# Feed-forward of a hash-attention block: units in a written issue order, without GpSimd

## The chip, the cores and the metric

The kernel runs on one core of a Trainium2 chip. The metric is the device time of one execution in microseconds (us). The core has TensorE (PE, matrix products; PEld is its loading of weights), VectorE (DVE), ScalarE (ACT), GpSimd (POOL) and SyncE (SP), each with its own queue of instructions that it runs in order. SBUF is the memory that all engines work on, PSUM the one that TensorE writes its products to.

## The reference

Four batches of eight heads, 768 positions of 64 numbers. Each query and each key gets a 6-bit bucket from the signs of a projection, and a query attends only to keys of its own bucket. The result `x` of 3072 rows x 512 goes through a feed-forward of 2048 columns:

```python
h = x @ w_in                      # 3072 x 512 @ 512 x 2048
sp = np.maximum(h, 0.0) + np.log1p(np.exp(-np.abs(h)))
g = h * erf(sp)
return (g @ w_out).astype(np.float32)   # @ 2048 x 512
```

## The kernel before

Everything is in float32. Attention comes first (lines 85 to 374): for each head and each 128 queries `attend` makes scores, maximum, exponential and normalized weights, `turn` transposes the weights on TensorE with the matrix `ident` and copies them out of PSUM on ScalarE, and `weigh` multiplies with the values and writes `xT`, the transposed input of the feed-forward, which stays in SBUF. The weights `w_in` and `w_out` come in meanwhile and stay in SBUF too.

The feed-forward (from line 376) takes the rows in 12 tiles of T = 256, and each tile's 2048 columns in NG = 4 groups of 512. One tile and group is a *unit* `u`; there are NU = 48. All tiles of a unit's arithmetic are 128 partitions x 1024 numbers. The steps of a unit, by function:

- `hidden` (L391): the first product, 16 products of 128 x 256 into `h_ps`, a PSUM tile of two banks. The trace has two records for each product, so 32 records.
- `take` (L406): ScalarE copies `h_ps` to `h` (L410), which frees the PSUM buffer; VectorE makes `e` = |h| (L411).
- `exponential` (L419): ScalarE `e` = exp(-e) (L423), VectorE `w` = (e + 1) - 1 (L424).
- `softplus` (L428): ScalarE `s` = Ln(e + 1) (L433), GpSimd `w` = e - w (L434, what the rounding of e + 1 lost), VectorE `s` = max(h, 0) + s (L435) and `s` = min(s, 4) + w (L438).
- `polynomial` (L442): erf is written as a Tanh of a polynomial, a product of three factors. ScalarE squares `s` into `z` (L446), then for each factor squares `z` plus a constant from `cq` (L450), and VectorE adds a constant and multiplies (L451).
- `gate` (L457): ScalarE Tanh (L460), GpSimd `h` = h * tanh (L461).
- `project` (L465): the second product. For a tile and 128 of its rows (`tt` 0 or 1), `half` says which two groups are added into `o_ps`: 8 products, 16 records, of 128 x 512. After the second half VectorE copies the result out (L480) and SyncE sends it to memory.

The first product has two PSUM buffers of two banks (`ps_h`), the second four of one bank (`ps_o`). They lie where attention's PSUM pools lay: `ps_sc` (scores, two of two banks), `ps_t` (transposes and hash bits, three banks) and `ps_av` (one bank).

The loop over pairs of units (L491 on) writes `hidden`, `project`, `take` and `polynomial` of the pair before, then `exponential`, `gate`, `softplus`. This text order is only a priority. A planner, which holds an estimated duration for each operation, decides at compile time in which order each engine issues what is ready, so a later unit's step can stand ahead of an earlier one's. ScalarE loads a table of functions (ACT_TABLE_LOAD) when a function is not in the one loaded; in the trace Ln needs another one than exp and Tanh, and copy and square need none.

Of the kernel before, what the change touches and what calls it, by code (L numbers as in the profile page):

```python
# [29 lines left out]
F32 = mybir.dt.float32  # L33
# [3 lines left out]
AF = mybir.ActivationFunctionType  # L37
ALU = mybir.AluOpType
AX = mybir.AxisListType
PSUM = bass.MemoryType.PSUM  # L40

P = 128
# [4 lines left out]
ERF_LEAD = 1.418517747371711e-07  # L47
ERF_Q = (
    (6.2794604751645355, 19.35174303303216),
    (-5.316226701641483, 239.37499811839012),  # L50
    (-20.943483610527835, 66.98472325796595),
)
# [3 lines left out]
def kernel(  # L56
# [11 lines left out]
    nc = tc.nc  # L68
# [10 lines left out]
    T = 256  # L79
    G = 4  # L80
    NG = NF // G
    TPB = S // T
    scale = 1.0 / D**0.5
    assert D == 64 and S == 768 and DM == H * D and NT == B * S and 1 << (NB2 // 2) == P - D

    const = ctx.enter_context(tc.tile_pool(name="const", bufs=1))
    ident = const.tile([P, P], F32, name="ident")
    make_identity(nc, ident)
    proj_sb = const.tile([P, NB2], F32, name="proj_sb")
    powers_f = const.tile([NB2, 2 * D], F32, name="powers_f")  # L90
    powers_b = const.tile([NB2, 2 * D], BF16, name="powers_b")
# [22 lines left out]
    ]  # L114

    with (
        tc.tile_pool(name="load", bufs=4) as load,
        tc.tile_pool(name="bitp", bufs=2) as bitp,
        tc.tile_pool(name="ep", bufs=4) as ep,
# [5 lines left out]
        tc.tile_pool(name="ps_t", bufs=3, space=PSUM) as ps_t,  # L125
        tc.tile_pool(name="ps_av", bufs=1, space=PSUM) as ps_av,
    ):
        heads = {}

        def fetch(i):  # L130
# [219 lines left out]
        for n in range(NH * NC + 3):  # L350
# [16 lines left out]
            w = n - 3  # L367
# [4 lines left out]
            t = n - 2  # L372
# [3 lines left out]
    cq = const.tile([P, len(ERF_Q)], F32, name="cq")  # L376
    for j, (c, _) in enumerate(ERF_Q):
        nc.vector.memset(cq[:, j : j + 1], c)

    hp = ctx.enter_context(tc.tile_pool(name="hp", bufs=8))  # L380
    ew = ctx.enter_context(tc.tile_pool(name="ew", bufs=2))
    sp = ctx.enter_context(tc.tile_pool(name="sp", bufs=4))
    work = ctx.enter_context(tc.tile_pool(name="work", bufs=2))
    outp = ctx.enter_context(tc.tile_pool(name="outp", bufs=2))
    ps_h = ctx.enter_context(tc.tile_pool(name="ps_h", bufs=2, space=PSUM))
    ps_o = ctx.enter_context(tc.tile_pool(name="ps_o", bufs=4, space=PSUM))

    NU = (NT // T) * NG
    st = {}

    def hidden(u):  # L391
        t, g = divmod(u, NG)
        b, t0 = t // TPB, (t % TPB) * T
        ps = ps_h.tile([P, G, T], F32, name="h_ps", tag="h")
        for f in range(G):
            for kc in range(NK):
                nc.tensor.matmul(  # L397
                    out=ps[:, f, :],
                    lhsT=w_in_sb[:, kc, (g * G + f) * P : (g * G + f + 1) * P],
                    rhs=xT[b][:, kc, t0 : t0 + T],  # L400
                    start=(kc == 0),
                    stop=(kc == NK - 1),
                )
        st[u] = dict(ps=ps)

    def take(u):  # L406
        d = st[u]
        h = d["h"] = hp.tile([P, G, T], F32, name="h", tag="h")
        e = d["e"] = ew.tile([P, G, T], F32, name="e", tag="e")
        nc.scalar.copy(out=h, in_=d.pop("ps"))  # L410
        nc.vector.tensor_scalar(  # L411
            out=e[:, :, :].bitcast(I32),
            in0=h[:, :, :].bitcast(I32),
            scalar1=0x7FFFFFFF,
            scalar2=None,
            op0=ALU.bitwise_and,
        )

    def exponential(u):  # L419
        d = st[u]  # L420
        e = d["e"]
        w = d["w"] = ew.tile([P, G, T], F32, name="w", tag="w")
        nc.scalar.activation(out=e, in_=e, func=AF.Exp, scale=-1.0)  # L423
        nc.vector.tensor_scalar(  # L424
            out=w, in0=e, scalar1=1.0, scalar2=-1.0, op0=ALU.add, op1=ALU.add
        )

    def softplus(u):  # L428

        d = st[u]  # L430
        h, e, w = d["h"], d.pop("e"), d.pop("w")
        s = d["s"] = sp.tile([P, G, T], F32, name="s", tag="s")
        nc.scalar.activation(out=s, in_=e, func=AF.Ln, bias=1.0)  # L433
        nc.gpsimd.tensor_tensor(out=w, in0=e, in1=w, op=ALU.subtract)  # L434
        nc.vector.scalar_tensor_tensor(  # L435
            out=s, in0=h, scalar=0.0, in1=s, op0=ALU.max, op1=ALU.add
        )
        nc.vector.scalar_tensor_tensor(  # L438
            out=s, in0=s, scalar=S_MAX, in1=w, op0=ALU.min, op1=ALU.add
        )  # L440

    def polynomial(u):  # L442
        d = st[u]
        p = d.pop("s")
        z = work.tile([P, G, T], F32, name="z", tag="z")
        nc.scalar.activation(out=z, in_=p, func=AF.Square)  # L446
        for j, (_, r) in enumerate(ERF_Q):
            last = j == len(ERF_Q) - 1
            q = z if last else work.tile([P, G, T], F32, name=f"q{j}", tag=f"q{j}")
            nc.scalar.activation(out=q, in_=z, func=AF.Square, bias=cq[:, j : j + 1])  # L450
            nc.vector.scalar_tensor_tensor(  # L451
                out=q, in0=q, scalar=r, in1=p, op0=ALU.add, op1=ALU.mult
            )
            p = q
        d["p"] = p

    def gate(u):  # L457
        d = st[u]
        p = d.pop("p")
        nc.scalar.activation(out=p, in_=p, func=AF.Tanh, scale=ERF_LEAD)  # L460
        nc.gpsimd.tensor_tensor(out=d["h"], in0=d["h"], in1=p, op=ALU.mult)  # L461

    o_live = {}

    def project(t, half, tt):  # L465

        if half == 0:
            o_live[tt] = ps_o.tile([P, DM], F32, name="o_ps", tag="o")
        ps = o_live[tt]
        for f in range(half * NF // 2, (half + 1) * NF // 2):  # L470
            nc.tensor.matmul(  # L471
                out=ps,
                lhsT=st[t * NG + f // G]["h"][:, f % G, tt * P : (tt + 1) * P],
                rhs=w_out_sb[:, f, :],
                start=(f == 0),
                stop=(f == NF - 1),
            )
        if half == 1:
            ob = outp.tile([P, DM], F32, name="ob", tag="ob")
            nc.vector.tensor_copy(out=ob, in_=ps)  # L480
            r0 = t * T + tt * P
            nc.sync.dma_start(out=out[r0 : r0 + P, :], in_=ob)
        if tt == 1:
            for g in range(half * NG // 2, (half + 1) * NG // 2):
                st.pop(t * NG + g)

    NB = NU // 2
    for k in range(NB + 2):
        for j in range(2):
            if k < NB:  # L490
                hidden(2 * k + j)  # L491
            if k >= 2:
                project((k - 2) // 2, (k - 2) % 2, j)
            if k < NB:
                take(2 * k + j)
            if 1 <= k <= NB:
                polynomial(2 * (k - 1) + j)
        for j in range(2):
            if k < NB:
                exponential(2 * k + j)  # L500
        for j in range(2):
            if 1 <= k <= NB:
                gate(2 * (k - 1) + j)
        for j in range(2):
            if k < NB:
                softplus(2 * k + j)


# [51 lines left out]
```

## Time and profile before

| | us |
|---|---|
| Median of 3 runs | 1537.13 |
| Lowest and highest | 1536.66 and 1537.61 |
| The profiled execution | 1537.1 |
| Its span (first to last instruction) | 1535.3 |
| Mean granted clock of TensorE | 0.985 |

| Engine | busy us | share of the span |
|---|---|---|
| PE | 1435.7 | 94% |
| PEld | 805.3 | 52% |
| DVE | 1080.8 | 70% |
| ACT | 874.9 | 57% |
| POOL | 379.0 | 25% |

Shares over the whole span mix attention and feed-forward, which have different limits; a table by stage separates them. "Idle before, releaser" behind a row says how long the engine stood still before that work and what ended its wait. [...] Several instructions of one kind in a row are merged into one line with their count (x32).

### The profile page before, as it was taken

Reading aid. Unit: us, or ns where it says so; the run is one execution under the profiler, and the core shown is the slowest. Engines: PE = TensorE matmul, PEld = TensorE weight load, DVE = VectorE, ACT = ScalarE, POOL = GpSimd, SP = SyncE. Lnnn points to the kernel's source line nnn. Section 1 sums busy time; section 2 is a strip of 40 time slices with the busy share of each in tenths; the row PEclk is TensorE's granted clock in tenths of the full one; section 3 lists DMA queues with packets and bytes.
Section 4 is the critical chain, followed back from the end, with each engine's and each line's share of the span. In section 5 each row is a group of like instructions: output and inputs, shape, how many; then the busy total and the mean of one; then the engine's idle time right before and its main releaser. Section 6 shows DMA issues by size and latency. Waiting matters only on the chain.

```text
span 1535.3 us, 14770 instructions
## 1 busy us (share of the span) xinstructions
PE 1435.7 (94%) x5248; PEld 805.3 (52%) x5248; DVE 1080.8 (70%) x1772; ACT 874.9 (57%) x1249; POOL 379.0 (25%) x198
## 2 busy tenths in 40 slices
PE   7999999999999999999997999989898999998986
PEld 3444444444444444544575666656565656565552
DVE  6888878888786676676638766666666665665673
ACT  2444444444444454454548877676767776676764
POOL 3333323332220000000014433333232323323231
PEclk9999999999999999999998999999999999999998
DMA  5222222222211011010000000000000000000000
GB/s 154 80 64 67 67 74 81 70 67 64 67 36 42 26 37 41 26 37 6 1 0 1 7 7 14 7 7 14 1 14 7 7 14 1 14 7 7 14 7 20
DMA packets 40705, 49.19 MB, mean 32 GB/s; under 512 B 27308, under 2 KB 27320, under 8 KB 40632
## 3 DMA queue, kind: packets, MB, share of 16 engines
q1 hardware_dynamic: 35856, 31.47, 6.9%
q0 software_dynamic: 4608, 16.78, 3.5%
q8 instruction: 41, 0.67, 0.2%
q14 instruction: 32, 0.26, 0.1%
q10 hardware_dynamic: 168, 0.01, 0.0%
HBM read 41.96 MB, written 6.29 MB: 31 GB/s over the span
## 4 chain that ended last, share of the span: by engine, by line
PE 37%; DVE 27%; ACT 26%; issue 7%; POOL 2%; DMA 1%; POOLq 0%; SPq 0%; DVEq 0%; ACTq 0%
PE av L332 13%; PE sc L274 11%; DVE s L435 7%; PE tr_ps L317 7%; ACT q L450 5%; DVE s L438 3%; ACT e L423 3%; ACT z L446 3%; DVE m L282 3%; ACT L433 3%; DVE q L451 2%; ACT h L410 2%; PE bits_ps L225 2%; ACT L460 2%; ACT s L433 2%
## 5 line engine op out<-in xcount | busy, mean ns | idle before, releaser
L397 PE MATMUL h_ps<-xT,w_in_sb 128*128 128x256 f32 x1536 | 349.0, 386 | 44.1 <-ACT h L410 43.9
L471 PE MATMUL o_ps<-w_out_sb,h 128*128 128x512 f32 x768 | 344.3, 602 | 22.4 <-POOL h L461 22.4
L397 PEld LDWEIGHTS h_ps<-xT,w_in_sb 128*128 128x128 f32 x1536 | 293.6, 193 | 115.9 <-ACT h L410 69.9
L324 ACT COPY eT<-tr_ps 128x384 f32<-128x384 f32 x384 | 171.0, 481 | 319.2 <-PE tr_ps L317 317.8
L274 PE MATMUL sc<-ka,qa 128*128 128x384 f32 x768 | 299.0, 498 | 11.0 <-ACT e L289 10.3
L332 PE MATMUL av<-eT,vt 128*64 128x384 f32 x768 | 261.6, 490 | 0.0
L471 PEld LDWEIGHTS o_ps<-w_out_sb,h 128*128 128x128 f32 x768 | 148.1, 193 | 192.5 <-issue 164.5
L434 POOL TENSOR_TENSOR w<-e,w 128x1024 f32<-128x1024 f32 x48 | 114.7, 2389 | 487.1 <-DVE w L424 487.1
L282 DVE TENSOR_REDUCE m<-sc 128x1 f32<-128x768 f32 x192 | 183.2, 954 | 64.5 <-PE sc L274 61.4
L289 ACT ACTIVATE e<-sc,nm 128x768 f32<-128x768 f32 x192 | 173.9, 906 | 90.4 <-DVE nm L284 87.9
L461 POOL TENSOR_TENSOR h<-h,z 128x1024 f32<-128x1024 f32 x48 | 119.8, 2497 | 357.2 <-ACT z L460 357.2
L317 PEld LDWEIGHTS tr_ps<-ident,e 128*128 128x128 f32 x1152 | 126.2, 140 | 120.5 <-issue 50.6
L317 PE MATMUL tr_ps<-ident,e 128*128 128x128 f32 x1152 | 176.9, 281 | 7.2 <-DVE e L302 2.4
L332 PEld LDWEIGHTS av<-eT,vt 128*64 128x64 f32 x768 | 99.8, 137 | 153.2 <-issue 145.2
L274 PEld LDWEIGHTS sc<-ka,qa 128*128 128x128 f32 x768 | 126.5, 192 | 69.1 <-ACT e L289 25.4
L435 DVE SCALAR_TENSOR_TENSOR s<-h,s 128x1024 f32<-128x1024 f32 x48 | 118.5, 2468 | 37.2 <-ACT s L433 37.2
L446 ACT ACTIVATE z<-s 128x1024 f32<-128x1024 f32 x48 | 50.7, 1056 | 157.6 <-DVE s L438 157.6
L451 DVE SCALAR_TENSOR_TENSOR q<-q,s 128x1024 f32<-128x1024 f32 x48 | 62.8, 1308 | 91.3 <-ACT q L450 91.3
L302 DVE TENSOR_SCALAR e<-e,r 128x768 f32<-128x768 f32 x192 | 124.3, 648 | 2.8
L424 DVE TENSOR_SCALAR w<-e 128x1024 f32<-128x1024 f32 x48 | 66.7, 1389 | 73.4 <-ACT e L423 73.4
L450 ACT ACTIVATE q<-z,cq 128x1024 f32<-128x1024 f32 x96 | 105.1, 1140 | 1.4
L339 DVE COPY xT<-av 64x384 f32<-64x384 f32 x64 | 35.3, 551 | 92.6 <-PE av L332 92.5
(44 smaller groups left out, 1227.2 us busy)
## 6 DMA issues: line engine op xcount, KB each, us to landing
qa<-in_qkT_dram SPq DMA_DIRECT2D x32, 384.0 KB, 3.4
raw<-in_w_in_dram POOLq DMA_DIRECT2D x16, 512.0 KB, 4.2
raw<-in_w_out_dram POOLq DMA_DIRECT2D x16, 512.0 KB, 3.8
ka<-in_qkT_dram SPq DMA_DIRECT2D x32, 192.0 KB, 3.8
vt<-in_v_dram SPq DMA_DIRECT2D x32, 192.0 KB, 2.5
out_dram<-ob SPq DMA_DIRECT2D x24, 256.0 KB, 2.0
powers_f<-in_powers_dram ACTq DMA_DIRECT2D x1, 6.0 KB
proj_sb<-in_proj_dram SPq DMA_DIRECT2D x1, 6.0 KB, 1.7
```

The costliest lines, as they stand in the source:

```text
L274: nc.tensor.matmul(out=sc[:, half, 0:HS], lhsT=d["qa"][:, c * P : (c + 1) * P], rhs=d["ka"][:, half * HS : (half + 1) * HS], start=True, s ...
L282: nc.vector.reduce_max(out=m, in_=sc[:, :, 0:HS], axis=AX.XY)
L289: nc.scalar.activation(out=e[:, :].rearrange("p (h k) -> p h k", h=2), in_=sc[:, :, 0:HS], func=AF.Exp, bias=nm[:, 0:1], scale=scale, accu ...
L302: nc.vector.tensor_scalar(out=e, in0=e, scalar1=r[:, 0:1], scalar2=None, op0=ALU.mult)
L317: nc.tensor.transpose(out=ps[:, j * P : (j + 1) * P], in_=e[:, kc * P : (kc + 1) * P], identity=ident,)
L324: nc.scalar.copy(out=dst, in_=src)
L332: nc.tensor.matmul(out=av[rows, :], lhsT=d["vt"][:, kc, :], rhs=d["eT"][:, kc, :], start=(kc == 0), stop=(kc == NC - 1),)
L397: nc.tensor.matmul(out=ps[:, f, :], lhsT=w_in_sb[:, kc, (g * G + f) * P : (g * G + f + 1) * P], rhs=xT[b][:, kc, t0 : t0 + T], start=(kc = ...
L435: nc.vector.scalar_tensor_tensor(out=s, in0=h, scalar=0.0, in1=s, op0=ALU.max, op1=ALU.add)
L450: nc.scalar.activation(out=q, in_=z, func=AF.Square, bias=cq[:, j : j + 1])
L461: nc.gpsimd.tensor_tensor(out=d["h"], in0=d["h"], in1=p, op=ALU.mult)
L471: nc.tensor.matmul(out=ps, lhsT=st[t * NG + f // G]["h"][:, f % G, tt * P : (tt + 1) * P], rhs=w_out_sb[:, f, :], start=(f == 0), stop=(f ...
```

## The change

1. `ident` moves from the pool that stays to a pool `one` that is released with attention.
2. `e - w` and `h * tanh` move from GpSimd to VectorE; the first now stands in `exponential`, directly behind `w`.
3. `polynomial` takes both units of a pair, factor by factor. It multiplies into `s` in place, and `q1` shares its two buffers (tag `wq`) with `w`. `e`, `w`/`q1`, `z` and `q0` have two buffers each, `h` nine in place of eight, `s` five in place of four.
4. `ps_h` has three buffers (six banks), `ps_o` two.
5. The loop is written in periods `p` of one pair and stands in `manual_schedule()`: within it each engine issues its instructions in the order of the text. Where these fall among the instructions outside it (the end of attention) is still the planner's. A pair has its first products in period p (the second one's `take` follows in p+1), exponential and `softplus` in p+1, the polynomial in p+2, `gate` and `project` in p+3.

```diff
-    ident = const.tile([P, P], F32, name="ident")
-    make_identity(nc, ident)
...
+        tc.tile_pool(name="one", bufs=1) as one,
...
+        ident = one.tile([P, P], F32, name="ident")
+        make_identity(nc, ident)
...
-    hp = ctx.enter_context(tc.tile_pool(name="hp", bufs=8))
-    ew = ctx.enter_context(tc.tile_pool(name="ew", bufs=2))
-    sp = ctx.enter_context(tc.tile_pool(name="sp", bufs=4))
+    hp = ctx.enter_context(tc.tile_pool(name="hp", bufs=9))
+    sp = ctx.enter_context(tc.tile_pool(name="sp", bufs=5))
...
-    ps_h = ctx.enter_context(tc.tile_pool(name="ps_h", bufs=2, space=PSUM))
-    ps_o = ctx.enter_context(tc.tile_pool(name="ps_o", bufs=4, space=PSUM))
+    ps_h = ctx.enter_context(tc.tile_pool(name="ps_h", bufs=3, space=PSUM))
+    ps_o = ctx.enter_context(tc.tile_pool(name="ps_o", bufs=2, space=PSUM))
...
+    NP = NU // 2
...
-        e = d["e"] = ew.tile([P, G, T], F32, name="e", tag="e")
+        e = d["e"] = work.tile([P, G, T], F32, name="e", tag="e")
...
-        w = d["w"] = ew.tile([P, G, T], F32, name="w", tag="w")
+        w = d["w"] = work.tile([P, G, T], F32, name="w", tag="wq")
...
+        nc.vector.tensor_tensor(out=w, in0=e, in1=w, op=ALU.subtract)
...
-        nc.gpsimd.tensor_tensor(out=w, in0=e, in1=w, op=ALU.subtract)
...
-    def polynomial(u):
-        d = st[u]
-        p = d.pop("s")
-        z = work.tile([P, G, T], F32, name="z", tag="z")
-        nc.scalar.activation(out=z, in_=p, func=AF.Square)
+    def polynomial(us):
+        for u in us:
+            st[u]["z"] = work.tile([P, G, T], F32, name="z", tag="z")
+            nc.scalar.activation(out=st[u]["z"], in_=st[u]["s"], func=AF.Square)
         for j, (_, r) in enumerate(ERF_Q):
-            last = j == len(ERF_Q) - 1
-            q = z if last else work.tile([P, G, T], F32, name=f"q{j}", tag=f"q{j}")
-            nc.scalar.activation(out=q, in_=z, func=AF.Square, bias=cq[:, j : j + 1])
-            nc.vector.scalar_tensor_tensor(
-                out=q, in0=q, scalar=r, in1=p, op0=ALU.add, op1=ALU.mult
-            )
-            p = q
-        d["p"] = p
+            for u in us:
+                z, s = st[u]["z"], st[u]["s"]
+                if j == 0:
+                    q = work.tile([P, G, T], F32, name="q0", tag="q0")
+                elif j == 1:
+                    q = work.tile([P, G, T], F32, name="q1", tag="wq")
+                else:
+                    q = z
+                nc.scalar.activation(out=q, in_=z, func=AF.Square, bias=cq[:, j : j + 1])
+                nc.vector.scalar_tensor_tensor(
+                    out=s, in0=q, scalar=r, in1=s, op0=ALU.add, op1=ALU.mult
+                )
...
-        p = d.pop("p")
-        nc.scalar.activation(out=p, in_=p, func=AF.Tanh, scale=ERF_LEAD)
-        nc.gpsimd.tensor_tensor(out=d["h"], in0=d["h"], in1=p, op=ALU.mult)
+        s = d.pop("s")
+        nc.scalar.activation(out=s, in_=s, func=AF.Tanh, scale=ERF_LEAD)
+        nc.vector.tensor_tensor(out=d["h"], in0=d["h"], in1=s, op=ALU.mult)
...
-    def project(t, half, tt):
-
+    def project(k, tt):
+
+        t, half = divmod(k, NG // 2)
...
-    NB = NU // 2
-    for k in range(NB + 2):
-        for j in range(2):
-            if k < NB:
-                hidden(2 * k + j)
-            if k >= 2:
-                project((k - 2) // 2, (k - 2) % 2, j)
-            if k < NB:
-                take(2 * k + j)
-            if 1 <= k <= NB:
-                polynomial(2 * (k - 1) + j)
-        for j in range(2):
-            if k < NB:
-                exponential(2 * k + j)
-        for j in range(2):
-            if 1 <= k <= NB:
-                gate(2 * (k - 1) + j)
-        for j in range(2):
-            if k < NB:
-                softplus(2 * k + j)
+    with tc.manual_schedule():
+        for p in range(NP + 3):
+            if p < NP:
+                hidden(2 * p)
+            if 1 <= p <= NP:
+                take(2 * p - 1)
+            if p >= 3:
+                gate(2 * p - 6)
+                gate(2 * p - 5)
+            if 1 <= p <= NP:
+                exponential(2 * p - 2)
+                exponential(2 * p - 1)
+                softplus(2 * p - 2)
+                softplus(2 * p - 1)
+            if p < NP:
+                take(2 * p)
+            if 2 <= p <= NP + 1:
+                polynomial((2 * p - 4, 2 * p - 3))
+            if p >= 3:
+                project(p - 3, 0)
+            if p < NP:
+                hidden(2 * p + 1)
+            if p >= 3:
+                project(p - 3, 1)
```

## Rows read from the trace of the kernel before

**Rows 1.** Busy time by stage (x instructions), last three: PEclk, DMA share, GB/s
```profile
784.00:1531.00 747.00, 680.54 (x2294) 439.72 (x2292) 489.08 (x359) 524.13 (x480) 234.44 (x96) 0.97 0.02 9
...
900.00:1000.00 100.00, 100.00 (x346) 65.36 (x344) 67.21 (x49) 68.90 (x64) 31.27 (x13) 1.00 0.02 8
1100.00:1200.00 100.00, 90.08 (x310) 58.21 (x309) 66.01 (x49) 67.32 (x62) 31.91 (x14) 1.00 0.03 11
```

**Rows 2.** Waits of PE from 776 us on: total, times, longest
```profile
PE h_ps L397 <- ACT h L410: 43.9, 28, 3.4
PE o_ps L471 <- POOL h L461: 22.4, 4, 8.8
```

**Rows 3.** Timeline of one round of the loop: start, us, engine, line
```profile
1079.35 0.99 ACT L410 COPY h<-h_ps 128x1024 f32<-128x1024 f32 x1
...
1080.39 7.17 PE L397 MATMUL h_ps<-xT,w_in_sb 128*128 128x256 f32 x32 [1.54 <-ACT h L410]
1081.06 0.69 DVE L411 TENSOR_SCALAR e<-h 128x1024 int32<-128x1024 int32 x1
...
1085.77 2.35 POOL L434 TENSOR_TENSOR w<-e,w 128x1024 f32<-128x1024 f32 x1 [0.63 <-DVE w L424]
1086.06 3.14 DVE L435 SCALAR_TENSOR_TENSOR s<-h,s 128x1024 f32<-128x1024 f32 x1 [0.36 <-ACT s L433]
...
1090.56 1.06 ACT L446 ACTIVATE z<-s 128x1024 f32<-128x1024 f32 x1 [4.54 <-DVE s L438]
...
1095.97 7.17 PE L397 MATMUL h_ps<-xT,w_in_sb 128*128 128x256 f32 x32 [1.53 <-ACT h L410]
```

**Rows 4.** Timeline of PE where it does not wait
```profile
834.95 7.07 PE L397 MATMUL h_ps<-xT,w_in_sb 128*128 128x256 f32 x32
841.86 7.03 PE L471 MATMUL o_ps<-w_out_sb,h 128*128 128x512 f32 x16
848.73 7.07 PE L397 MATMUL h_ps<-xT,w_in_sb 128*128 128x256 f32 x32
```

**Rows 5.** Timeline where attention ends: first product's records there
```profile
776.16 1.10 PE L397 MATMUL h_ps<-xT,w_in_sb 128*128 128x256 f32 x4
...
783.20 33.07 PE L397 MATMUL h_ps<-xT,w_in_sb 128*128 128x256 f32 x152
```

**Rows 6.** Timeline at the end of the span
```profile
1531.42 0.69 DVE L480 COPY ob<-o_ps 128x512 f32<-128x512 f32 x1 [6.18 <-PE o_ps L471]
```

**Rows 7.** Timeline of PE after its longer waits
```profile
828.48 6.63 PE L471 MATMUL o_ps<-w_out_sb,h 128*128 128x512 f32 x8 [8.77 <-POOL h L461]
...
1143.39 7.17 PE L397 MATMUL h_ps<-xT,w_in_sb 128*128 128x256 f32 x32 [3.40 <-ACT h L410]
...
1268.70 10.14 PE L397 MATMUL h_ps<-xT,w_in_sb 128*128 128x256 f32 x32 [3.40 <-ACT h L410]
```

**Rows 8.** Groups by line: busy us, mean ns, idle before and releaser
```profile
L435 DVE SCALAR_TENSOR_TENSOR s<-h,s 128x1024 f32<-128x1024 f32 x48 | 118.5, 2468 | 37.2 <-ACT s L433 37.2
...
L450 ACT ACTIVATE q<-z,cq 128x1024 f32<-128x1024 f32 x96 | 105.1, 1140 | 1.4
...
L433 ACT ACT_TABLE_LOAD x48 | 61.6, 1283 | 0.8
L451 DVE SCALAR_TENSOR_TENSOR z<-z,q 128x1024 f32<-128x1024 f32 x48 | 60.7, 1264 | 5.3 <-DVE q L451 0.9 <-ACT z L450 0.8
L438 DVE SCALAR_TENSOR_TENSOR s<-s,w 128x1024 f32<-128x1024 f32 x48 | 58.8, 1224 | 4.6
...
L433 ACT ACTIVATE s<-e 128x1024 f32<-128x1024 f32 x48 | 50.7, 1057 | 0.5
...
L460 ACT ACT_TABLE_LOAD x38 | 48.8, 1283 | 0.7
...
L410 ACT COPY h<-h_ps 128x1024 f32<-128x1024 f32 x48 | 47.7, 993 | 12.8 <-PE h_ps L397 12.8
...
L480 DVE COPY ob<-o_ps 128x512 f32<-128x512 f32 x24 | 16.3, 681 | 13.5 <-PE o_ps L471 13.5
...
L423 ACT ACT_TABLE_LOAD x10 | 12.8, 1283 | 4.3 <-DVE e L411 4.2
```

More of the change, by code (lines that the diff above doesn't have):

```diff
@@ L477, in project @@
             )
-        if half == 1:
+        if half == NG // 2 - 1:
             ob = outp.tile([P, DM], F32, name="ob", tag="ob")
@@ L483, in project @@
         if tt == 1:
-            for g in range(half * NG // 2, (half + 1) * NG // 2):
-                st.pop(t * NG + g)
-    NB = NU // 2
-    for k in range(NB + 2):
-        for j in range(2):
-            if k < NB:
-                hidden(2 * k + j)
-            if k >= 2:
-                project((k - 2) // 2, (k - 2) % 2, j)
-            if k < NB:
-                take(2 * k + j)
-            if 1 <= k <= NB:
-                polynomial(2 * (k - 1) + j)
-        for j in range(2):
-            if k < NB:
-                exponential(2 * k + j)
-        for j in range(2):
-            if 1 <= k <= NB:
-                gate(2 * (k - 1) + j)
-        for j in range(2):
-            if k < NB:
-                softplus(2 * k + j)
+            st.pop(2 * k)
+            st.pop(2 * k + 1)
+    assert T == 2 * P
+    with tc.manual_schedule():
[22 more added lines that the diff above has]
+                project(p - 3, 1)
 _OUT = ((3072, 512), "float32")
```

## The prediction

> **What bounds the kernel now.** I read the stage table first: the feed-forward holds the span from 784 to 1531 us [rows 1]. In it TensorE is busy 680.5 of 747 us, VectorE 489 and ScalarE 524. So TensorE is the engine with most work, yet it stands still. One stretch, 900 to 1000 us, has TensorE at 100.00 and the granted clock at 1.00, while the stretch 1100 to 1200 has 90.08. The engines can therefore feed it, and the order usually doesn't.
>
> The table of waits says for what TensorE stands: 43.9 us in 28 waits on the copy that empties `h_ps` (L410) and 22.4 us in 4 waits on GpSimd's product (L461) [rows 2]. The timeline shows the loop behind the 28 [rows 3]. ScalarE's queue has the copy of a unit behind the square of L446. That square waited 4.54 us for VectorE's `s`. VectorE's first step towards `s` (L435) took 3.14 us, because it ran beside GpSimd's 2.35 us subtraction. The copy ends at 1080.34, and the first product, which had waited 1.54 us for the buffer, starts at 1080.39. The next starts at 1095.97, so a unit goes round in 15.58 us.
>
> Without a wait, one first product and the second product of one unit take 848.73 - 834.95 = 13.78 us, 6.91 and 6.87 [rows 4]. 48 of them are 661.4 us, against 748.2 between 783.20, when attention's last product is out of the way [rows 5], and 1531.4, when the last copy of a result starts [rows 6]. The gap of about 87 us is what an order can give back at most: 66.3 us of waits, and some 20 us of a lowered clock after them. After a wait of 3.40 us one unit of 32 records took 10.14 us, after another of 3.40 only 7.17, and after one of 8.77 us 8 records of the second product took 6.63 us, where 3.5 is the full pace [rows 7]. [...]
>
> **The change, part by part.** TensorE's own work is the same: 48 x 13.78. The question is whether, in the written order, anything is late for it in a period. A period is two first products and two projections, 27.56 us. Its start is 0: `hidden(2p)` 0 to 6.9, `project(p-3,0)` to 13.8, `hidden(2p+1)` to 20.7, `project(p-3,1)` to 27.6.
>
> *ScalarE.* Per unit: the copy 0.99, exp, Ln, square and Tanh about 1.06 each, three biased squares of 1.14 [rows 8]. That is 8.65, and 17.3 for two units. Table loads are 1.28. Ln has one for each of the 48 units now; Tanh has 38, and a further 10 stand at exp, so exp and Tanh share one load [rows 8]. The written order puts two Tanh, two exp and two Ln side by side: two loads in a period in place of four. Sum 19.9 us of 27.56.
>
> *VectorE.* The two GpSimd operations of a unit come to it. The trace has no such two-input fp32 subtraction or product on VectorE. The nearest below is a one-input step at 0.69 [rows 3], the nearest above the mean of L435, 2.47, and its twin in shape, L438, costs 1.22 [rows 8]. I take 1.22, as L438 has two inputs of the same size and no GpSimd beside it, and keep 0.69 and 2.47 as ends. The period is 4 x 0.69 + 4 x 1.22 (moved) + 4 x 1.22 (L435, L438) + 6 x 1.26 (L451) = 20.1, and 0.68 on average for the copies of L480 (two in every second period): 20.8 us. With the moved four at 2.47 it is 25.8, still under 27.56. The cover is 2 us or more.
>
> *L435.* It falls from 2.47 to about 1.22 if it was GpSimd that lengthened it. [...]
>
> *Does anything come late?* `hidden(2p-1)` ends 6.9 before 0. Then ScalarE: copy to -5.8, load and two Tanh to -2.3 (their input is the polynomial of the period before). VectorE: |h|, then the two gate products, done at -2.1 and -0.9. `project(p-3,0)` wants the first at +6.9 and the second 3.4 later. So there are 9 us to spare. In every second period VectorE has a result copy for `project(k,1)` at the end of its queue, and this one blocks it until 27.6 + 0.7. The next period's |h| and gate products stand behind it: 0.9 + 0.69 + 1.22 = 2.8 and 4.1. TensorE still has 4 us to spare for the first, because `hidden(2p)` covers it. The rest of that period's VectorE work ends at 20.8, so the delay is gone by the next. ScalarE's second copy, `take(2p)`, goes at 6.9 to 8.1, behind the two Ln (done at 3 in a free period, 6.1 in a blocked one); its buffer is wanted at 13.8 of the next period. The other buffers (`h` 9, `s` 5, `e`, `z`, `q0` and the shared `wq` 2) all come free before they are wanted. Steady state: no wait, 27.56 a period.
>
> *Start.* The order needs three periods before the first projection. In the third, ScalarE copies unit 4 only when `hidden(4)` ends at 34.4 us from the start, and the polynomial of units 0 and 1 stands behind it: squares to 45.3, VectorE's last steps to 46.5 and 47.8, load and Tanh to 48.9, first gate product to 50.1. `hidden(6)` ends at 48.2: a wait of 2.0 us. In the kernel before the start costs 8.77 [rows 7].
>
> *Junction.* Now 8 records of the first product (160 less 152, 1.7 us) fit into TensorE's pauses while attention ends [rows 5]. The third `h_ps` buffer lies where attention's transposes have theirs until their last copies, so these records can come later. Between 0 and 1.7 us lost; I take 1.7, as the whole pool may wait, and count the feed-forward from 783.2.
>
> *End.* In the periods with no first product, TensorE has only 13.78 us. VectorE enters the first of them late, at -6.7, with 20.1 us of work and the two result copies before it comes to the next gate product, which ends at 17.8; TensorE was free at 13.8: a wait of 4.0. The last pair's gate comes at 29.1, before TensorE's 31.6. A wait of 4 us is longer than the 3.40 after which the clock fell in one case and not in the other: 10.14 - 7.17 = 3.0 or nothing; I take 2.
>
> *Sum.* 783.2 + 661.4 + 2.0 + 4.0 + 2 = 1452.6. From TensorE's end to the span's end: the last result copy starts at 1531.42 of 1535.3, so 3.9 [rows 6]: 1456.5. The profiled execution takes 1537.1 with a span of 1535.3, 1.8 outside: 1458.3. It agrees with the median of 1537.13, so no shift. Forecast 1458.
>
> *Ends.* No loss at junction, start and end: 781.5 + 661.4 + 3.9 + 1.8 = 1448.6. The moved operations at 2.47: start +4 (two subtractions and a product ahead of the first gate), end +6 (three or four of them), so 1468; with some 5 us more from attention's end being ordered otherwise and a second fall of the clock (3.0), 1476. With 0.69, some 3 less. The forecast's range is 1448 to 1476.
>
> **Rivals.** *A wait stays in each period.* The order is in-order on every engine, so one late item, such as the gate product behind VectorE's blocked result copy, stops TensorE each time. For: VectorE is blocked in 12 periods, with only 4 us to spare. Against: ScalarE and VectorE have some 7 us a period free. With today's 1.54 us once a period: 24 x 1.54 = 37, so 1495. Chance 0.09 (1476 to 1515).
>
> *Nothing changes.* The 15.58 us loop is one of dependencies that the order only moves: 24 x 31.16 = 748, 1537. Against it, the polynomial no longer waits for an `s` made in the same period, and the copies stand ahead of it. 0.02.
>
> *VectorE becomes the bound, and it is slower.* The place is VectorE's queue in each period: were its two-input operations to cost 2.47 without GpSimd too, 14 x 2.47 + 4 x 0.69 + 0.68 = 38.0 a period, 24 of them 912, so 748 becomes 912 and the time 1701. It decides from 748 / 24 = 31.2 us a period, which is 1.98 an operation. For it: L435's mean. Against: L438 and L451 have two inputs too and stay at 1.22 and 1.26. 0.03.
>
> **How the numbers follow.** Forecast 0.86, the rivals 0.09, 0.02 and 0.03. The range of 1448 to 1476 leaves 0.14 out. Faster by over 0.2% (3 us, about what a measurement of this kernel tells from none) is the forecast and the first rival: 0.95; same 0.02, slower 0.03.
>
> **What would show it.** Right: TensorE near 100% with clock 1.00 from about 835 to 1400, first products 27.5 us apart by pairs, no entry of `h_ps` on L410's copy in its waits, two entries for the gate product (2 and 4 us), L435 at 1.22, 48 or 49 table loads in the feed-forward. Wrong: a wait of TensorE that comes back each period or each second period, the moved operations well over 1.22, or an attention stage that ends elsewhere than at 783.

## The result, and the profile after

1457.79 us, median of 4 runs (1457.63 to 1458.18), against 1537.37 for the kernel before: ratio 0.9483, 95% interval 0.9466 to 0.9499. The profiled execution took 1457.63 with a span of 1455.9. The forecast was 1458, the range 1448 to 1476.

The stage table of the changed kernel, with the columns of [rows 1]: from 834 to 1400 us TensorE is busy for 565.99 of 566 us, at a granted clock of 1.00.

```profile
834.00:1400.00 566.00, 565.99 (x1971) 374.57 (x1972) 406.62 (x396) 388.46 (x375) 0.00 (x0) 1.00 0.03 10
...
1100.00:1200.00 100.00, 100.00 (x348) 65.82 (x347) 74.10 (x73) 69.20 (x68) 0.00 (x0) 1.00 0.02 8
```

TensorE's waits from 770 us on, for [rows 2]: the 28 on the copy are gone, two on the gate product are left, and the second line still belongs to attention.

```profile
PE o_ps L477 <- DVE h L466: 3.6, 2, 2.9
PE tr_ps L319 <- DVE e L304: 1.9, 2, 1.1
```

TensorE's timeline of the changed kernel. The first row answers to [rows 5], the second and the last show the two waits, and the rows between answer to [rows 4].

```profile
784.72 48.61 PE L399 MATMUL h_ps<-xT,w_in_sb 128*128 128x256 f32 x224
834.01 7.10 PE L477 MATMUL o_ps<-w_out_sb,h 128*128 128x512 f32 x16 [0.67 <-DVE h L466]
840.95 7.07 PE L399 MATMUL h_ps<-xT,w_in_sb 128*128 128x256 f32 x32
...
1391.88 7.07 PE L399 MATMUL h_ps<-xT,w_in_sb 128*128 128x256 f32 x32
...
1422.48 29.43 PE L477 MATMUL o_ps<-w_out_sb,h 128*128 128x512 f32 x64 [2.93 <-DVE h L466]
```

From 840.95 to 1391.88 lie 40 units, 13.77 us each, which is the pace without a wait. The groups by line, for [rows 8]:

```profile
L430 DVE TENSOR_TENSOR w<-e,w 128x1024 f32<-128x1024 f32 x48 | 58.8, 1225 | 1.7
...
L437 DVE SCALAR_TENSOR_TENSOR s<-h,s 128x1024 f32<-128x1024 f32 x48 | 58.5, 1219 | 0.0
L466 DVE TENSOR_TENSOR h<-h,s 128x1024 f32<-128x1024 f32 x48 | 56.6, 1221 | 16.7 <-ACT s L465 16.7
...
L436 ACT ACT_TABLE_LOAD x24 | 30.8, 1283 | 0.4
L465 ACT ACT_TABLE_LOAD x23 | 29.5, 1283 | 0.4
...
L426 ACT ACT_TABLE_LOAD x1 | 1.3, 1283 | 0.0
```

The moved operations cost 1.22 us. The first step towards `s` (L435 before, L437 now) fell from 2.47 to 1.22 though nothing of it was edited. The table loads of the feed-forward are 48 in place of 96.

One period in which VectorE was blocked by the result copy, from the changed kernel's timeline:

```profile
1102.64 7.07 PE L399 MATMUL h_ps<-xT,w_in_sb 128*128 128x256 f32 x32
1102.84 0.69 DVE L486 COPY ob<-o_ps 128x512 f32<-128x512 f32 x1 [9.16 <-PE o_ps L477]
...
1104.05 2.35 DVE L466 TENSOR_TENSOR h<-h,s 128x1024 f32<-128x1024 f32 x2
...
1109.55 7.03 PE L477 MATMUL o_ps<-w_out_sb,h 128*128 128x512 f32 x16
```

VectorE stood for 9.16 us behind the copy of L486. Both gate products still ended at 1106.4, 3.8 us into the period, before the projection at 1109.55.

### The profile page after: what moved, and what is told of

Its sections match the earlier page's. It is cut to its first block, busy times and chain, and to the rows that moved or that the text cites. A ratio compares the mean times of both kernels' runs of the same rounds, so it can differ in the third digit from the quotient of the medians.

```text
span 1455.9 us, 14558 instructions
## 1 busy us (share of the span) xinstructions
PE 1418.3 (97%) x5248; PEld 803.2 (55%) x5248; DVE 1058.9 (73%) x1868; ACT 799.2 (55%) x1201; POOL 144.5 (10%) x102
## 4 chain that ended last, share of the span: by engine, by line
PE 79%; DVE 14%; ACT 2%; issue 2%; POOL 1%; DMA 1%; SPq 0%; ACTq 0%; POOLq 0%; DVEq 0%
PE o_ps L477 21%; PE h_ps L399 21%; PE av L334 14%; PE sc L276 12%; PE tr_ps L319 7%; DVE m L284 3%; PE bits_ps L227 2%; DVE e L304 2%; ACT e L291 1%; DVE qa L254 1%; PE bucket_ps L246 1%; DVE top L197 1%; DVE keep L170 1%; DVE ka L262 1%; DMA qa<-in_qkT_dram 1%
## 5 line engine op out<-in xcount | busy, mean ns | idle before, releaser
L477 PE MATMUL o_ps<-w_out_sb,h 128*128 128x512 f32 x768 | 338.5, 595 | 3.6 <-DVE h L466 3.6
L399 PE MATMUL h_ps<-xT,w_in_sb 128*128 128x256 f32 x1536 | 338.5, 379 | 0.0
L412 ACT COPY h<-h_ps 128x1024 f32<-128x1024 f32 x48 | 48.5, 1011 | 171.3 <-PE h_ps L399 171.3
L458 DVE SCALAR_TENSOR_TENSOR s<-q,s 128x1024 f32<-128x1024 f32 x96 | 111.1, 1220 | 23.0 <-ACT q L457 23.0
L457 ACT ACTIVATE q<-z,cq 128x1024 f32<-128x1024 f32 x96 | 102.1, 1134 | 0.0
L486 DVE COPY ob<-o_ps 128x512 f32<-128x512 f32 x24 | 16.5, 690 | 109.3 <-PE o_ps L477 109.3
L173 POOL TENSOR_SCALAR keep<-keep 128x512 int32<-128x512 int32 x32 | 73.2, 2287 | 92.8 <-DVE nm L286 56.8
L466 DVE TENSOR_TENSOR h<-h,s 128x1024 f32<-128x1024 f32 x48 | 56.6, 1221 | 16.7 <-ACT s L465 16.7
L413 DVE TENSOR_SCALAR e<-h 128x1024 int32<-128x1024 int32 x48 | 33.1, 690 | 45.0 <-ACT h L412 45.0
```

Of the source, the lines that this page charges most:

```text
L173: nc.gpsimd.tensor_scalar(out=keep, in0=keep, scalar1=float((1023 - 126) << 20), scalar2=-1.0, op0=ALU.is_ge, op1=ALU.mult,)
L399: nc.tensor.matmul(out=ps[:, f, :], lhsT=w_in_sb[:, kc, (g * G + f) * P : (g * G + f + 1) * P], rhs=xT[b][:, kc, t0 : t0 + T], start=(kc = ...
L458: nc.vector.scalar_tensor_tensor(out=s, in0=q, scalar=r, in1=s, op0=ALU.add, op1=ALU.mult)
L477: nc.tensor.matmul(out=ps, lhsT=st[t * NG + f // G]["h"][:, f % G, tt * P : (tt + 1) * P], rhs=w_out_sb[:, f, :], start=(f == 0), stop=(f ...
```

## The experiments

They ask which part of the change carries the 80 us: the written order and its depth (O, later D), the end of GpSimd's part in the loop (G), or the third `h_ps` buffer (B). The kernel before was run beside each, with medians of 1537.7 to 1537.8.

**The changed kernel without the written order**

```diff
-    with tc.manual_schedule():
+    if True:
```

> The changed kernel without the written order: the same text, but the planner orders each engine. Theory O (the written order removes the loop of 15.58 us a unit, in which the copy out of h_ps stood behind squares that waited for an s made in the same period): TensorE's waits on the copy come back in part, over 1480 us. Rival G (GpSimd made the loop long; without it the loop is 15.58 - (3.14 - 1.22) = 13.66 us, under TensorE's 13.78): the order does not matter, 1455 to 1465.

1459.26 us, ratio 0.9487 (0.9471 to 0.9502). The planner's order on the new text does as well as the written one. It has one wait of TensorE in the feed-forward, 4.1 us at the start. So O as it was stated is wrong.

**The changed kernel with GpSimd's two operations**

```diff
-        nc.vector.tensor_tensor(out=w, in0=e, in1=w, op=ALU.subtract)
+        nc.gpsimd.tensor_tensor(out=w, in0=e, in1=w, op=ALU.subtract)
...
-        nc.vector.tensor_tensor(out=d["h"], in0=d["h"], in1=s, op=ALU.mult)
+        nc.gpsimd.tensor_tensor(out=d["h"], in0=d["h"], in1=s, op=ALU.mult)
```

> The changed kernel with the subtraction and the gate product on GpSimd again, 2.35 us each, in the written order. Theory O: in a period VectorE's own work is 20.8 - 4.9 = 15.9 us, lengthened by GpSimd's at most by 4 x 2.35 = 9.4 to 25.3, under 27.56, and the gate product of 2.35 still ends before TensorE wants it: 1457 to 1468, the rest from start and end. Rival G: the lengthened L435 and the product bring waits back in each period, 1490 or more.

1465.23 us, 0.9531 (0.9517 to 0.9545). The groups by line show VectorE lengthened again:

```profile
L440 DVE SCALAR_TENSOR_TENSOR s<-s,w 128x1024 f32<-128x1024 f32 x48 | 105.7, 2202 | 5.4 <-DVE s L437 0.5
...
L427 DVE TENSOR_SCALAR w<-e 128x1024 f32<-128x1024 f32 x48 | 85.5, 1802 | 46.3 <-ACT e L426 46.3
L437 DVE SCALAR_TENSOR_TENSOR s<-h,s 128x1024 f32<-128x1024 f32 x48 | 84.1, 1752 | 0.0
```

The stage table shows that TensorE does not notice:

```profile
834.00:1380.00 546.00, 545.24 (x1887) 359.23 (x1888) 405.93 (x298) 373.80 (x360) 216.71 (x82) 1.00 0.03 10
```

Its two waits at start and end are 10.5 us in place of 3.6. That is most of the 7 us more. So G alone isn't the cause of the gain either.

**The kernel before with the two operations on VectorE, nothing else**

```diff
-        nc.gpsimd.tensor_tensor(out=w, in0=e, in1=w, op=ALU.subtract)
+        nc.vector.tensor_tensor(out=w, in0=e, in1=w, op=ALU.subtract)
...
-        nc.gpsimd.tensor_tensor(out=d["h"], in0=d["h"], in1=p, op=ALU.mult)
+        nc.vector.tensor_tensor(out=d["h"], in0=d["h"], in1=p, op=ALU.mult)
```

> The kernel before with one edit: the subtraction and the gate product on VectorE in place of GpSimd; planner's order, two h_ps buffers. Theory O: the loop of the copy stays, with L435 shorter the unit takes some 14.5 us or more: over 1490. Rival G: the loop falls to 13.66 us, so TensorE is the bound and the waits of L397 on the copy are nearly gone: 1460 to 1480.

1457.26 us, 0.9478 (0.9464 to 0.9493), a little under G's range: two words of the kernel give the whole gain. Its timeline, in a round with the order of [rows 3]:

```profile
1116.80 0.99 ACT L410 COPY h<-h_ps 128x1024 f32<-128x1024 f32 x1
...
1120.50 7.07 PE L397 MATMUL h_ps<-xT,w_in_sb 128*128 128x256 f32 x32
...
1122.06 1.23 DVE L434 TENSOR_TENSOR w<-e,w 128x1024 f32<-128x1024 f32 x1
...
1123.52 1.23 DVE L435 SCALAR_TENSOR_TENSOR s<-h,s 128x1024 f32<-128x1024 f32 x1 [0.23 <-ACT s L433]
...
1126.03 1.06 ACT L446 ACTIVATE z<-s 128x1024 f32<-128x1024 f32 x1 [2.55 <-DVE s L438]
...
1130.40 0.99 ACT L410 COPY h<-h_ps 128x1024 f32<-128x1024 f32 x1
```

The square waits 2.55 us for `s` in place of 4.54. From copy to copy it takes 13.60 us, where G had 13.66; that is just under TensorE's 13.78, and the first product at 1120.50 shows no wait. Other rounds take 12.3 to 16.8 us, as the planner's order and the result copies fall. Eight of them, from the copy at 1088.00 to the one at 1198.21, average 13.78, which is TensorE's own pace. In the kernel before, eight average 15.66 (1063.77 to 1189.08).

**The kernel before with three `h_ps` buffers**

```diff
-    ps_h = ctx.enter_context(tc.tile_pool(name="ps_h", bufs=2, space=PSUM))
-    ps_o = ctx.enter_context(tc.tile_pool(name="ps_o", bufs=4, space=PSUM))
+    ps_h = ctx.enter_context(tc.tile_pool(name="ps_h", bufs=3, space=PSUM))
+    ps_o = ctx.enter_context(tc.tile_pool(name="ps_o", bufs=2, space=PSUM))
```

> The kernel before with three h_ps buffers and two o_ps buffers, GpSimd and planner as they were. Theories O and G: a loop of 15.58 us a unit is not shortened by a buffer, 1525 to 1540. Rival B (the waits on the copy are for want of a buffer): the 28 waits go, 1537 - 44 = 1493 or less.

1542.57 us, 1.0032 (1.0019 to 1.0045), 0.3% slower and a little over the range expected. TensorE's waits have changed their name only: none on the copy of `h_ps`, but 61.1 us on the result copy, which frees the two `o_ps` buffers that are left.

```profile
PE o_ps L471 <- DVE ob L480: 61.1, 14, 12.1
PE o_ps L471 <- POOL h L461: 8.8, 1, 8.8
```

The edit also takes two `o_ps` buffers away. That this doesn't hide a gain is seen in ScalarE's loop, which goes as before. Its wait for `s` is as long, in the kernel before (first) and here:

```profile
L446 ACT ACTIVATE z<-s 128x1024 f32<-128x1024 f32 x48 | 50.7, 1056 | 157.6 <-DVE s L438 157.6
```

```profile
L446 ACT ACTIVATE z<-s 128x1024 f32<-128x1024 f32 x48 | 50.7, 1056 | 157.5 <-DVE s L438 157.5
```

Its copies still come 15.58 us apart:

```profile
1081.08 0.99 ACT L410 COPY h<-h_ps 128x1024 f32<-128x1024 f32 x1
...
1096.66 0.99 ACT L410 COPY h<-h_ps 128x1024 f32<-128x1024 f32 x1
```

So B is wrong: the loop set the pace, and the buffer only chose where TensorE stands.

**One operation moved at a time, in the kernel before**

```diff
-        nc.gpsimd.tensor_tensor(out=w, in0=e, in1=w, op=ALU.subtract)
+        nc.vector.tensor_tensor(out=w, in0=e, in1=w, op=ALU.subtract)
```

> The kernel before with the subtraction alone on VectorE, the gate product still on GpSimd. Theory L (the loop of the copy is a chain whose length sets the unit): w (L424) still ends at 1085.69 beside the gate product, the subtraction then takes 1.22 in place of 2.35 and L435 is no longer lengthened; s is ready 1.1 us earlier, so 15.58 becomes 14.5 us, 0.7 over TensorE's 13.78: 1457 + 48 x 0.7 = 1491. Rival C (any relief of GpSimd is enough): 1457 to 1465. Rival N (only both together help): over 1525.

```diff
-        nc.gpsimd.tensor_tensor(out=d["h"], in0=d["h"], in1=p, op=ALU.mult)
+        nc.vector.tensor_tensor(out=d["h"], in0=d["h"], in1=p, op=ALU.mult)
```

> The kernel before with the gate product alone on VectorE, the subtraction still on GpSimd. Theory L: w is no longer lengthened (2.00 to 0.69), but the product of 1.22 stands ahead of it, GpSimd's subtraction ends about 1.0 us earlier and L435 with it: 15.58 becomes 14.6, 1457 + 48 x 0.85 = 1498. Rival C: 1457 to 1465. Rival N: over 1525.

1506.73 us (0.98, 0.9786 to 0.9815) with the subtraction moved, 1494.9 (0.9719, 0.9703 to 0.9735) with the gate product moved. Both lie in between, as L has it, 31 and 43 us under the kernel before, where both moves together give 80. The second was 3 us off and the first 16. In the first, a round in the order of [rows 3] takes 14.52 us, as L has it, so the miss lies in the other rounds, up to 16.57 us. Its timeline has a place there that L's working left out: beside the gate product on GpSimd, |h| (L411) takes 2.09 us in place of 0.69, and exp waits for it.

```profile
1158.11 2.35 POOL L461 TENSOR_TENSOR h<-h,z 128x1024 f32<-128x1024 f32 x1 [14.02 <-ACT z L460]
1158.91 2.09 DVE L411 TENSOR_SCALAR e<-h 128x1024 int32<-128x1024 int32 x1 [2.02 <-ACT h L410]
...
1161.04 1.06 ACT L423 ACTIVATE e<-e 128x1024 f32<-128x1024 f32 x1 [2.16 <-DVE e L411]
```

**Depth alone: the changed kernel with GpSimd and without the written order.** The edits are those of the first and the second experiment together.

> The changed kernel with both operations on GpSimd and without the written order (the planner orders). Theory D (a polynomial one period behind its s takes the chain out of the loop, in whatever order): 1462 to 1475, as with the written order (1465). Rival W (with GpSimd in it the loop needs the written order): over 1490.

1464.52 us, 0.9527 (0.9512 to 0.9541). D holds: with the polynomial a period behind its `s`, GpSimd may stay in, in whichever order. ScalarE's wait for `s` ahead of the first square, 157.6 us in the kernel before, is 6.5:

```profile
L447 ACT ACTIVATE z<-s 128x1024 f32<-128x1024 f32 x48 | 50.0, 1045 | 6.5 <-DVE s L440 6.5
```

This kernel has 96 table loads in the feed-forward, as many as the kernel before, so the loads that the written order saves are not what it takes. The new text also takes the two units of a pair factor by factor and has other numbers of buffers; with GpSimd in the loop these were not tried apart from the depth.

**The changed kernel with the PSUM buffers of before**

```diff
-    ps_h = ctx.enter_context(tc.tile_pool(name="ps_h", bufs=3, space=PSUM))
+    ps_h = ctx.enter_context(tc.tile_pool(name="ps_h", bufs=2, space=PSUM))
...
-    ps_o = ctx.enter_context(tc.tile_pool(name="ps_o", bufs=2, space=PSUM))
+    ps_o = ctx.enter_context(tc.tile_pool(name="ps_o", bufs=4, space=PSUM))
```

> The changed kernel with two h_ps and four o_ps buffers, as before the change. The prediction's timetable: a copy is done 5.7 us before its buffer is wanted even with two, and the first product's records fit into attention's last pauses again (1.7 us): 1455 to 1458. Rival B (the third buffer carries the gain): waits on the copy come back, 1480 or more.

1454.22 us, 0.9458 (0.9444 to 0.9472), a little under the range expected, with no wait on a copy of `h_ps`. The third buffer is not needed. Two of its four runs, 1452.65 and 1452.85, had a mean granted clock of 0.999, the other two, 1455.59 and 1456.13, one of 0.995.

**More VectorE work in the changed kernel**: the room that the prediction saw. `spare` is a bf16 tile in a pool of its own that nothing reads; the second kernel has 4 operations in place of 2. Each takes 1.225 us.

```diff
         nc.vector.tensor_tensor(out=w, in0=e, in1=w, op=ALU.subtract)
+        for _ in range(2):
+            nc.vector.tensor_tensor(out=spare, in0=e, in1=w, op=ALU.add)
```

> The changed kernel with two more two-input VectorE operations of 1.22 us in each unit (their result is not used): 4.9 us a period on top of about 20, so 25 of TensorE's 27.55. The prediction's statement that such work is covered in the steady state: no wait between 834 and 1400, about 4 us more at the start and up to 10 at the end, 1463 to 1476. Rival V (VectorE, blocked in each second period by the result copy, had no such room): a wait in each second period, over 1480.

> The changed kernel with four more two-input VectorE operations in each unit: 9.8 us a period, 29.6 or more in all, over TensorE's 27.55. VectorE becomes the bound: 24 x 2 = 49 us and 10 to 20 at start and end, 1505 to 1540, with waits of TensorE on VectorE in most periods. Were ScalarE's and VectorE's chain the bound already in the changed kernel, two and four more would cost in proportion (117 and 235 us).

With two, 1471.33 us (0.9563, 0.9547 to 0.9579). The stage table has VectorE at 86.70% and TensorE still at 100:

```profile
1100.00:1200.00 100.00, 100.00 (x352) 66.63 (x351) 86.70 (x84) 67.15 (x64) 0.00 (x0) 1.00 0.03 11
```

The two waits at start and end are 14.7 us in place of 3.6. With four, 1531.62 us (0.9957, 0.9942 to 0.9972). VectorE is the bound, 538 of 546 us, and the gate product comes late for TensorE:

```profile
834.00:1380.00 546.00, 509.29 (x1733) 330.94 (x1734) 538.44 (x502) 349.91 (x336) 0.00 (x0) 0.97 0.02 9
```

```profile
1142.06 8.83 PE L481 MATMUL o_ps<-w_out_sb,h 128*128 128x512 f32 x16 [1.89 <-DVE h L470]
```

So the turn comes between 24 us of VectorE work a period (86.70% of 27.55) and 29 (4.9 more), where the working had it (27.55).

**A version with the end rearranged.** The edit is long; its core is the end of the loop, beside two `h_ps` and four `o_ps` buffers. `results()` makes the result copies that `project` now only notes, behind the gate products of the next period.

```diff
+        take(NU - 1)
+        gate(NU - 6)
+        gate(NU - 5)
+        results()
+        project(NP - 3, 0)
+        project(NP - 3, 1)
+        polynomial((NU - 4, NU - 3))
+        gate(NU - 4)
+        gate(NU - 3)
+        exponential(NU - 2)
+        exponential(NU - 1)
+        softplus(NU - 2)
+        softplus(NU - 1)
+        results()
+        project(NP - 2, 0)
+        project(NP - 2, 1)
+        polynomial((NU - 2, NU - 1))
...
```

> The changed kernel with two h_ps and four o_ps buffers, the result copies of a period behind the gate products of the next, and in the last periods the polynomial and gate of a pair ahead of the last pair's softplus. The prediction's end term: the wait of 2.9 us and the lowered clock behind it (1.9) go, and with the two h_ps buffers 1.7 us where attention ends: 1457.8 - 6.5 = 1451, between 1448 and 1454. If the end term was read wrongly: as with the buffers alone, 1454 to 1457.

> The changed kernel itself once more, on the chip of these three, so that they are compared with it there: 1456 to 1459.

1452.42 us (1452.08 to 1452.6; ratio 0.9443, 0.9428 to 0.9457). The changed kernel on the same chip: 1454.95 (1453.57 to 1457.93; 0.9462, 0.9448 to 0.9476), below its expectation. All runs of the new version lie under all of these, by 2.5 us at the medians, though the intervals of the two ratios overlap. What the end itself is worth is not shown: the buffers alone came to 1452.65 and 1452.85 in their two runs at a clock of 0.999, and all four runs of the new version had 0.999 or 1.000. The wait of 2.9 us is gone, and a smaller one, 1.77, stands at the last pair, whose softplus was put back:

```profile
1396.62 34.50 PE L486 MATMUL o_ps<-w_out_sb,h 128*128 128x512 f32 x80
1432.88 14.00 PE L486 MATMUL o_ps<-w_out_sb,h 128*128 128x512 f32 x32 [1.77 <-DVE h L466]
```

Where attention ends, its first product again starts with 4 records in a pause, as in [rows 5], and has 8 behind it when attention is through:

```profile
777.25 1.10 PE L399 MATMUL h_ps<-xT,w_in_sb 128*128 128x256 f32 x4
...
784.28 46.89 PE L399 MATMUL h_ps<-xT,w_in_sb 128*128 128x256 f32 x216
```

## Why the prediction was right

**The bound and its pace.** 48 x 13.78 = 661.4 was the main term. 13.77 was measured, with no wait in the steady state. The two sums behind it were somewhat high: a period is 27.55 us, so 834 to 1400 holds 20.5 of them, VectorE has 406.62 / 20.5 = 19.8 us (20.8 was worked out) and ScalarE 18.9 (19.9). One figure beside them was a slip: 25.8 leaves 1.8 us under 27.56, not 2.

**The small terms.**

| Term | predicted us | measured us |
|---|---|---|
| First product without attention from | 783.2 | 784.72 |
| Wait at the start | 2.0 | 0.67 |
| Wait at the end | 4.0 | 2.93 |
| Clock after it | 2 | 1.7 |
| From the last result copy to the span's end | 3.9 | 4.0 |

The two waits were forecast too long, in part because two steps in a row took a little less than twice one: two Tanh 2.00 us, not 2.12, and two gate products 2.36, not 2.44. At the start the first gate product began 47.9 us after 784.72, not 48.9. The clock's 1.7 is 29.43 less 27.73, the same 64 records after the same wait without a fall (below). The first row is scatter in part: with the same attention text and the written order the start was 782.54, 782.80, 783.52, 783.87 and 784.72 in five profiled executions, of which 783.52 and 784.72 are the changed kernel itself. The first term was 1.5 us more than forecast and the next three 2.7 less, so the exact 1458 is partly luck. That the 8 records no longer fit into attention's pauses (1.7 us) was right, and the two-buffer version shows it from the other side.

**The cause was told too narrowly.** The prediction called the 87 us "what an order can give back", and the runs don't bear out that step. The planner's order gives 1459 on the same text. What counts is the length of the chain from copy to copy, [rows 3], against 13.78 us. Two parts of the change each end TensorE's waits on the copy, and either is enough: VectorE in place of GpSimd (15.58 to 13.60 us for a round of that order, 1457), or the new text with the polynomial one period later (1465 with GpSimd in), in which the copies no longer stand behind a square that waits for an `s` of its own period. Together they give no more than the first alone. The prediction's own rows held that: 15.58 less the 1.92 us by which L435 was lengthened is 13.66, and 13.60 was measured.

**Rivals.** The first, a wait in each period behind VectorE's blocked result copy, did not come: the block is there, 9.16 us, and `hidden(2p)` covers it. The second, that the order only moves a loop of 15.58 us, did not come either, as TensorE's pace is 13.77 us a unit. The third, VectorE as the bound, needs some 8 us more work a period, and the kernel with four more operations a unit shows what it then does; a moved operation cost 1.22 us, not this rival's 2.47. That it was GpSimd that lengthened L435, the prediction's condition for it, agrees with the trace: its 2.47 us became 1.22 when GpSimd was out, and in the kernel with GpSimd put back it was 1.75 for that step and 2.20 for the next. By what means is not shown. The 1.22 us that the prediction took from L438 for the moved operations agrees too: 1.221 and 1.225 were measured.

## What to carry to other kernels

A wait of the bound engine on a buffer is first a question of the loop behind it: add up the chain from one release of the buffer to the next, and compare it with what the engine needs in that time, here 15.58 us with 13.78. Where that chain is the longer one, another buffer can just move the wait elsewhere, here 43.9 us on `h_ps` to 61.1 on `o_ps`. Compare the same place of the order in both kernels, or the mean of many rounds, since single rounds of one kernel took 12.3 to 16.8 us. Here each of two cuts that took the chain out of TensorE's way gave nearly everything, so try the smallest first: moving two operations off GpSimd was worth as much as the rewriting (1457.26 us and 1457.79).

## What the runs showed of the hardware

The same wait of TensorE was not always followed by the same clock. After 2.93 us the 64 last records took 29.43 us in the changed kernel and 27.73 in the version with two `h_ps` buffers, with a granted clock of 0.91 and 1.00 in the window from 1415 to 1435. The 0.91 is a mean of 0.85 from 1420 to 1425, 0.51 from 1425 to 1427 and 1.00 in the rest. The first row is the changed kernel's, the other two are the other's:

```profile
1415.00:1435.00 20.00, 17.07 (x36) 7.16 (x35) 17.81 (x17) 15.29 (x15) 0.00 (x0) 0.91 0.07 26
```

```profile
1415.00:1435.00 20.00, 17.07 (x40) 7.34 (x40) 14.54 (x14) 12.36 (x12) 0.00 (x0) 1.00 0.07 26
```

```profile
1419.20 27.73 PE L477 MATMUL o_ps<-w_out_sb,h 128*128 128x512 f32 x64 [2.93 <-DVE h L466]
```

The runs of one kernel scatter by up to 4 us (1453.57 to 1457.93); a fall that comes or not can make some 2 of these, by the 1.7 of these two. The two shorter of its four runs had a mean granted clock of 0.999 and 1.000, the two longer 0.995 and 0.996, so more of it may lie with the clock; that was not tried.
